# A hand-ordered attention and MLP kernel: loads of q, k, v and f shared between the DMA queues of SyncE and GpSimd, with a new order

## The chip, the cores and the metric

The kernel runs on one core of one Trainium2 chip. The metric is the device time of one execution in microseconds. A program is handed to the five engines as five instruction streams, each executed in order: TensorE (PE), VectorE (DVE), ScalarE (ACT), GpSimd (POOL) and SyncE (SP, which here only issues transfers). Semaphores tie the streams together. Transfers issued by SP go through one queue (q1 in the profile, hardware_dynamic), those issued by POOL through another (q0, software_dynamic); both are carried by the core's 16 transfer engines.

## What is computed

A gated linear attention (a state per head that decays by a sigmoid of f and takes in an outer product of k and v), and then an MLP with SiLU on its result:

```python
batch, n_heads, seq, head_dim = (4, 8, 768, 48)
f = 1.0 / (1.0 + np.exp(-f_logit))
for t in range(S):
    state = f[:, :, t, :, None] * state + np.einsum('bhd,bhe->bhde', k[:, :, t], v[:, :, t])
    y[:, :, t] = np.einsum('bhd,bhde->bhe', q[:, :, t], state)
x = y.transpose(0, 2, 1, 3).reshape(B * S, H * D)          # 3072 x 384
h = x @ w_in                                               # 384 -> 2048
out = (h * (1.0 / (1.0 + np.exp(-h)))) @ w_out             # 2048 -> 384
```

All inputs and the output are float32; the matmuls run in bfloat16.

## The kernel before

The sequence is cut into chunks of 128 steps, so there are 4 batches with 6 chunks each, 24 units. Two units are worked on together as a pair; there are twelve pairs, numbered P in the order of the list `PAIRS`. Pairs 0 to 3 hold chunks 0 and 1 of one batch (form T: a partition holds two neighbouring steps, so that a run in memory is 2 x 48 floats, 384 bytes). Pairs 4 to 11 hold the same chunk of two batches (form N: a run is 48 floats, 192 bytes). A load brings one of q, k, v, f for a whole pair, 384 KB, or half of it: 1024 runs for a T pair, 2048 for an N pair.

Within a chunk the recurrence is done by matmuls. E and L (ACT) make the logarithm of the gate from f, `cs` (PE) its running sum by a triangular matrix, `a`, `ia` and `al` (ACT) exponentials of it, `qg` and `ki` scaled copies of q and k, `vb` a bfloat16 copy of v. q and k are transposed either on PE (`tq`, copied out by `qkc`) or by a DMA transpose that SP issues (`qkD`). `sc` are the score matmuls, `at` their masking, `y` and `yi` the results from scores and from the state before, `d`, `sd` and `su` the state's update. `yc` copies y out, and y is transposed on PE (`yT`, `xc`) or by a DMA transpose (`yD`). The MLP of a pair has eight groups `mi` of six matmuls of 256 columns, each with a SiLU `si` on ACT, and two times four groups `mo` of four matmuls of 384 columns; `oc` copies a result out of PSUM and `so` stores it. The weights come by four loads `wi` and four `wo`, issued by POOL.

The order of all this on all engines is a written list, `PLAN`. A word such as `q.2.0:S:0` names the step (q), the pair (2), the part (0), the engine (A = ACT, V = DVE, G = POOL, S = SP, P = PE) and, after the second colon, the buffer that the step takes. The words are emitted in the order of the list, so each engine's stream is the list's words for it; nothing is reordered later. A step waits only for the data it reads and for the last use of the buffer that it takes, so a load whose buffer has not been used yet is issued as soon as its engine comes to it. The words `idle.512.n` put n filler matmuls on zeros onto PE (L424).

Every load of q, k, v and f is issued by SP:

```python
            return nc.sync.dma_start(out=dst, in_=src)     # L223
```

Its buffer comes from a pool of its own (`SLOTS`: f 4, k 6, q 6, v 6, of which the list uses two or three each). The first four loads of the list are emitted ahead of everything, then the masks are built on POOL and DVE, then the list follows.

Of the kernel before, what the change touches and what calls it, by code (L numbers as in the profile page):

```python
# [33 lines left out]
SLOTS = dict(f=4, k=6, q=6, v=6, e=2, lf=3, x=5, qk=5, vb=7, qkT=4, qkTT=2, atm=4, yb=3, xT=4, hT=4, sd=2, al=6, ob=6, pb=8, st0=1, st1=1, st2=1, st3=1)  # L34
# [23 lines left out]
at.3.0.0:V:0 si.2.7:A: mo.2.1.2:P: mo.2.1.3:P: vb.5.0:G:2 at.3.1.0:V:1 mo.2.0.0:P:3 mo.2.0.1:P: mo.2.0.2:P: f.4.0:S:1 E.4.0:A:0 sd.3.1:V:0 f.6.0:S:0
qkD.5.1:S:0 at.3.1.1:V: qkD.5.0:S:1 oc.2.1:A:4 L.4.0:A:0 cs.4.1:P:5 E.6.0:A:1 L.6.0:A:1 at.3.0.1:V: v.5.1:S: sc.5.0:P:7,6 y.3:P:0,4 sc.5.1:P:2,1
at.5.0.0:V:2 yi.3.1:P: a.4.1:A:0 yc.3.0:A:0 at.5.1.1:V:0 mo.2.0.3:P: at.5.0.1:V: yc.3.1:A:1 oc.2.0:A:5 al.4.1:A:1 d.5.0:P:0 cs.6.0:P:4 a.6.0:A:1  # L60
# [46 lines left out]
def kernel(  # L107
# [82 lines left out]
    def al_of(P, i):  # L190
        return at("al", P)[:, :, i] if PAIRS[P][0] == "T" else at("al", P, i)[:, :, 0]
# [5 lines left out]
    def emit(kind, rest, eng):  # L197
# [26 lines left out]
        if kind in "EL":  # L224
# [3 lines left out]
            if kind == "E":  # L228
                return nc.scalar.activation(e, at("f", P)[:, j * w:(j + 1) * w], AF.Exp, scale=-1.0)  # L229
# [276 lines left out]
```

## Time and profile before

| what | value |
|---|---|
| time, median of three runs | 181.08 us (178.41 to 182.14) |
| profiled execution: time, span | 178.94 us, 177.2 us |
| PE busy | 170.6 us, 96% |
| ACT busy | 130.4 us, 74% |
| DVE busy | 81.2 us, 46% |
| POOL busy | 62.5 us, 35% |
| moved by the transfer engines | 32.12 MB, 181 GB/s over the span |

The span is the time from the first to the last instruction in the trace; the execution's own time holds 1.7 us more. Matmuls are pipelined and their ends are modelled, so PE's busy time counts overlapping matmuls as busy and says little of how densely they follow each other: starts of neighbouring groups are the better measure. In a table of groups a line holds the source line, the engine, the operation, the number of instructions, the time they were busy and the mean of one in ns, and then the idle time before them and what ended it. In the chain of waits and in a timeline the first column is the start and the second the duration in us. In a view of the transfers a queue's line gives its packets, its megabytes and the time that its packets took as a share of 16 engines' time.

### The profile page before, as it was taken

Reading aid. Unit: us, or ns where it says so; the run is one execution under the profiler, and the core shown is the slowest. Engines: PE = TensorE matmul, PEld = TensorE weight load, DVE = VectorE, ACT = ScalarE, POOL = GpSimd, SP = SyncE. Lnnn points to the kernel's source line nnn. Section 1 sums busy time; section 2 is a strip of 40 time slices with the busy share of each in tenths; the row PEclk is TensorE's granted clock in tenths of the full one; section 3 lists DMA queues with packets and bytes.
Section 4 is the critical chain, followed back from the end, with each engine's and each line's share of the span. In section 5 each row is a group of like instructions: output and inputs, shape, how many; then the busy total and the mean of one; then the engine's idle time right before and its main releaser. Section 6 shows DMA issues by size and latency. Waiting matters only on the chain.

```text
span 177.2 us, 4721 instructions
## 1 busy us (share of the span) xinstructions
PE 170.6 (96%) x1912; PEld 124.7 (70%) x1915; DVE 81.2 (46%) x165; ACT 130.4 (74%) x241; POOL 62.5 (35%) x105
## 2 busy tenths in 40 slices
PE   6998999999999999999999999999999999999991
PEld 2446688666886788766787687686797686877860
DVE  7089751047795783125777174035770152520110
ACT  3968578953999989998499788899589574281721
POOL 6056593102383348400647323400471960000001
PEclk9999999999999999999999999999999999999999
DMA  5999999999999989997698796899968998132202
GB/s 145 301 311 256 213 225 204 188 179 237 218 196 201 211 177 199 219 204 151 135 231 152 148 228 141 213 192 212 234 129 191 212 150 242 48 91 87 93 0 89
DMA packets 110453, 32.12 MB, mean 181 GB/s; under 512 B 104080, under 2 KB 110256, under 8 KB 110432
## 3 DMA queue, kind: packets, MB, share of 16 engines
q1 hardware_dynamic: 106432, 27.89, 76.2%
q0 software_dynamic: 4000, 3.93, 12.2%
q8 instruction: 15, 0.25, 0.6%
q14 instruction: 6, 0.05, 0.1%
HBM read 25.17 MB, written 4.72 MB: 169 GB/s over the span
## 4 chain that ended last, share of the span: by engine, by line
PE 74%; ACT 9%; DVE 6%; DMA 4%; SPq 3%; issue 2%; DVEq 0%; ACTq 0%
PE pb L279 32%; PE pb L244 27%; DVE qk L312 3%; DMA q<-in_q_dram 3%; ACT hT L249 3%; PE pb L340 2%; ACT L473 2%; ACT x L307 2%; PE pb L352 2%; PE pb L356 2%; PE pb L336 1%; SPq L368 1%; DMA out_dram<-ob 1%; SPq L223 1%; PE pb L364 1%
## 5 line engine op out<-in xcount | busy, mean ns | idle before, releaser
L244 PE MATMUL pb<-xT,w_in_sb 128*128 128x256 bf16 x576 | 69.3, 272 | 0.5 <-ACT ob L180 0.2
L279 PE MATMUL pb<-w_out_sb,hT 128*128 128x384 bf16 x384 | 68.5, 326 | 0.0
L244 PEld LDWEIGHTS <-w_in_sb 128*128 128x128 bf16 x576 | 54.9, 98 | 9.6 <-issue 1.2
L249 ACT ACTIVATE hT<-pb 128x512 bf16<-128x512 f32 x96 | 50.5, 610 | 10.7 <-PE pb L244 10.5
L279 PEld LDWEIGHTS <-hT 128*128 128x128 bf16 x384 | 36.2, 98 | 21.0
L383 POOL TENSOR_TENSOR st<-sd,al 48x192 bf16<-48x192 f32 x40 | 21.7, 543 | 56.8 <-PE pb L352 34.2
L344 DVE TENSOR_TENSOR atm<-pb,triu 128x512 bf16<-128x512 f32 x32 | 20.1, 684 | 11.2 <-PE pb L340 6.6
L307 ACT ACTIVATE x<-pb 128x384 f32<-128x384 f32 x48 | 21.1, 497 | 5.2 <-PE pb L295 3.1
L473 ACT ACT_TABLE_LOAD x17 | 21.8, 1283 | 0.3
L182 DVE COPY ob<-pb 128x384 f32<-128x384 f32 x10 | 5.4, 552 | 26.6 <-PE pb L279 26.6
L377 DVE TENSOR_TENSOR sd<-pb,st 128x384 f32<-128x384 f32 x16 | 8.8, 553 | 11.8 <-PE pb L373 10.3
L312 POOL TENSOR_TENSOR qk<-k,x 128x384 bf16<-128x384 f32 x11 | 12.0, 1102 | 5.5 <-ACT x L307 2.4
L312 POOL TENSOR_TENSOR qk<-q,x 128x384 bf16<-128x384 f32 x11 | 10.9, 997 | 8.5 <-ACT x L307 5.5
L229 ACT ACTIVATE e<-f 128x768 f32<-128x768 f32 (+1 forms) x13 | 10.2, 792 | 4.8 <-DMA f<-in_f_logit_dram 4.8
L180 ACT COPY ob<-pb 128x384 f32<-128x384 f32 x14 | 6.7, 482 | 9.0 <-PE pb L279 8.2
L312 DVE TENSOR_TENSOR qk<-q,x 128x384 bf16<-128x384 f32 x13 | 8.6, 682 | 7.7 <-DMA q<-in_q_dram 4.2
L289 POOL DMA_DIRECT2D out_dram<-ob x3 | 1.7, 562 | 28.5 <-DVE ob L182 28.5
L424 PE MATMUL pb<-zero,triu 128*128 128x512 bf16 (+1 forms) x27 | 9.8, 463 | 1.5 <-POOL triu masks.py:66 1.4
L344 DVE TENSOR_TENSOR atm<-pb,mask 128x512 bf16<-128x512 f32 x16 | 10.2, 684 | 2.1 <-PE pb L336 1.0
L182 POOL CAST vb<-v 128x384 bf16<-128x384 f32 x12 | 6.5, 551 | 10.9 <-DMA v<-in_v_dram 10.5
L182 DVE CAST yb<-pb 128x384 bf16<-128x384 f32 x14 | 7.6, 555 | 5.4 <-PE pb L356 2.8
L180 ACT CAST yb<-pb 128x384 bf16<-128x384 f32 x10 | 4.8, 490 | 5.8 <-PE pb L356 4.3
(71 smaller groups left out, 148.8 us busy)
## 6 DMA issues: line engine op xcount, KB each, us to landing
f<-in_f_logit_dram SPq DMA_DIRECT2D x11, 384.0 KB, 5.2
k<-in_k_dram SPq DMA_DIRECT2D x10, 384.0 KB, 5.2
q<-in_q_dram SPq DMA_DIRECT2D x10, 384.0 KB, 5.4
v<-in_v_dram SPq DMA_DIRECT2D x10, 384.0 KB, 5.3
out_dram<-ob SPq DMA_DIRECT2D x13, 192.0 KB, 2.1
w_in_sb<-in_moe_w_in_dram POOLq DMA_DIRECT2D x4, 384.0 KB, 8.4
w_out_sb<-in_moe_w_out_dram POOLq DMA_DIRECT2D x4, 384.0 KB, 10.3
out_dram<-ob SPq DMA_DIRECT2D x14, 96.0 KB, 3.5
```

The costliest lines, as they stand in the source:

```text
L180: nc.scalar.copy(dst, src)
L182: ENG[eng].tensor_copy(dst, src)
L229: return nc.scalar.activation(e, at("f", P)[:, j * w:(j + 1) * w], AF.Exp, scale=-1.0)
L244: nc.tensor.matmul(h[:, i, cols], w_in_sb[:, kk, n * 128:(n + 1) * 128], at("xT", P)[:, kk, cols], start=(kk == 0), stop=(kk == KT - 1))
L249: return nc.scalar.activation(at("hT", P)[:, 2 * j:2 * j + 2, :], at("h", P, j).rearrange("p (n c) -> p n c", n=2), AF.Silu)
L279: nc.tensor.matmul(o, at("hT", P)[:, n, i * C:(i + 1) * C], w_out_sb[:, n, :], start=(n == 0), stop=(n == NT - 1))
L307: nc.scalar.activation(at(kind, P, i).rearrange("p h d -> p (h d)"), at("cs", P, i)[:, 0:HD], AF.Exp, scale=1.0 if kind == "ia" else -1.0)
L312: ENG[eng].tensor_mul(at("qk", P, i)[:, j, :, 0:D], heads("qk"[j], P, i), at("ia" if j else "a", P, i))
L344: ENG[eng].tensor_mul(at("atm", P, i)[:, r], at(f"s{r}", P, i).rearrange("p (n c) -> p n c", c=C), mask[:, None, :].to_broadcast([C, NP, C]))
L383: nc.gpsimd.tensor_mul(at("st", P, i)[lo:lo + D, :, r * D:(r + 1) * D], at("sd", P, i)[lo:lo + D, :, r * D:(r + 1) * D], al_of(P, i)[lo:lo ...
L424: nc.tensor.matmul(buf["pb", int(got)][:, 0:rest[0]], triu, zero[:, 0:rest[0]], start=True, stop=True, skip_group_check=True)
L473: nc.scalar.preload_act_table_set(turns[n])
```

## The change

All q, k, v and f loads take buffers from one pool of 24 (`inp`), and each word of the list says whether SP or POOL issues it. Of 55 such loads and halves of loads SP now issues 29 and POOL 26. The exponential E is written over f itself instead of a buffer e. The masks and the identity (`mk`, `mv`) and the column sums of the gates (`on`, formerly part of `cs`) are words of the list of their own. The state update `su` may run on DVE and does so for fourteen of twenty. Pairs 0 and 1 begin in the opposite order, POOL issues the most urgent loads of the first three pairs and the weights between them, and SP issues loads of later pairs from early on. PE's transposes `yT` fall from fifteen to six and DMA transposes `yD` rise from nine to eighteen. There are 24 filler matmuls (16 of 512 columns, 8 of 256) instead of 30 (26 and 4). POOL issues twelve of the 24 results' stores instead of four. Further words (`aD`, `ir`, a DMA transpose for T pairs) are defined and not used by this list.

The core of the diff (of the list: the beginnings, the stretch around the first N pairs, and the end):

```diff
-SLOTS = dict(f=4, k=6, q=6, v=6, e=2, lf=3, x=5, qk=5, vb=7, ...)
+SLOTS = dict(inp=24, lf=3, x=5, qk=5, vb=7, ...)
 PLAN = """
-f.1.0:S:0 E.1.0:A:0 L.1.0:A:0 idle.512.10::0 idle.256.1::0 cs.1.1:P:0 f.0.1:S:1 f.0.0:S: E.0.0:A:1 E.0.1:A: k.1.0:S:0 L.0.0:A:1 L.0.1:A: idle.512.1::1 cs.1.0:P:1
-q.1.0:S:0 idle.512.2::2 cs.0.0:P:2 idle.256.1::3 cs.0.1:P:3 a.1.1:A:0 qg.1.1:V:0 a.1.0:A:1 ia.1.1:A:2 ki.1.1:V: idle.512.1::4 tq.1.1:P:4 ia.1.0:A:3
-ki.1.0:V:1 v.1.0:S:0 f.2.0:S:0 qg.1.0:V: idle.512.3::5 tq.1.0:P:1 vb.1.1:V:0 vb.1.0:G:1 d.1:P:5,6 qkc.1.1:V:0 qkc.1.0:V: idle.512.1::7 idle.256.1::7
-sc.1.0:P:1,4 at.1.0.0:V:0 ia.0.0:A:0 k.0.0:S:1 ki.0.0:V:0 at.1.0.1:V: idle.512.2::7 idle.256.1::7 sc.1.1:P:7,1 at.1.1.0:V:1 at.1.1.1:V: a.0.1:A:2
-ia.0.1:A:3 sd.1.0:A:0 wi.1:G: al.1:A:0 E.2.0:A:1 L.2.0:A:1 q.0.0:S:1 a.0.0:A:1 qg.0.0:V: idle.512.1::5 cs.2.0:P:0 cs.2.1:P:5 al.2:A:1 ia.2.1:A:0
-su.1.0:G:0 ia.2.0:A:4 al.0:A:2 a.2.0:A:1 qg.0.1:V:1 idle.512.2::2 y.1:P:1,7 tq.0.0:P:4 v.0.0:S:1 yc.1.0:V:0 a.2.1:A:2 qkc.0.0:A:1 sd.1.1:V:0 wi.3:G:
-ki.0.1:G: tq.0.1:P:3 qkc.0.1:V: yT.1.0:P:1 yi.1.1:P: yc.1.1:A:0 wi.0:G: idle.512.2::2 sc.0.1:P:3,4 vb.0.1:G:0 at.0.1.0:V:0 yT.1.1:P:7 xc.1.0:A:0
-sc.0.0:P:6,5 at.0.0.1:V:1 at.0.0.0:V: vb.0.0:A:1 wi.2:G: idle.512.1::2 d.0:P:3,1 xc.1.1:A: sd.0.0:A:1 su.0.0:G:0 mi.1.2:P:7 mi.1.3:P:3 at.0.1.1:V:
-...
+f.0.1:S:0 E.0.1:A: f.0.0:S: E.0.0:A: L.0.0:A:0 L.0.1:A: f.1.0:G:1 E.1.0:A: L.1.0:A:1 mk.1:G: mk.0:G: mv.0:V: idle.512.9::0 idle.256.1::0 cs.0.1:P:0
+idle.256.1::1 cs.0.0:P:1 idle.256.1::2 on.0:P: idle.256.1::2 cs.1.0:P:2 cs.1.1:P:3 on.1:P: f.2.0:S:2 E.2.0:A: ia.1.0:A:0 a.1.0:A:1 L.2.0:A:1
+idle.512.4::4 cs.2.0:P:2 cs.2.1:P:4 q.1.0:G:3 qg.1.0:V:0 ia.1.1:A:2 k.1.0:G:4 a.1.1:A:1 ia.0.0:A:3 al.1:A:0 a.0.0:A:4 f.4.0:G:5 E.4.0:A: ki.1.0:V:
+mk.2:G: tq.1.0:P:5 ki.1.1:V:1 qg.1.1:V: on.2:P: tq.1.1:P:3 qkc.1.0:V:0 qkc.1.1:V: idle.512.2::6 idle.256.1::6 sc.1.0:P:3,5 ia.0.1:A:1 L.4.0:A:1
+al.0:A:1 a.0.1:A:2 k.0.0:G:0 v.1.0:G:1 vb.1.1:A:0 vb.1.0:A:1 al.2:A:2 sc.1.1:P:1,6 cs.4.0:P:7 cs.4.1:P:0 on.4.1:P: on.4.0:P: q.0.0:G:6 ki.0.1:V:2
+ia.2.1:A:1 wi.1:G: at.1.0.1:V:0 v.0.0:G:4 at.1.0.0:V: a.2.1:A:0 idle.512.1::5 d.1:P:3,5 sd.1.0:A:0 qg.0.1:V: wi.0:G: ki.0.0:G:3 k.2.0:G:5 ia.2.0:A:2
+tq.0.1:P:4 qkc.0.1:A:1 a.2.0:A:3 qg.0.0:G: tq.0.0:P:3 at.1.1.0:V:1 at.1.1.1:V: y.1:P:6,1 yc.1.0:A:0 su.1.0:V:0 yi.1.1:P: qkc.0.0:V: idle.256.1::4
+sc.0.0:P:3,4 yc.1.1:A:1 sd.1.1:V:0 idle.256.1::2 yT.1.0:P:6 idle.256.1::2 yT.1.1:P:1 q.2.0:G:1 wi.2:G: at.0.0.1:V:0 vb.0.1:G:0 xc.1.0:V:0 at.0.0.0:V:
+al.4.0:A:3 sc.0.1:P:5,2 at.0.1.1:V:1 at.0.1.0:V: vb.0.0:A:1 d.0:P:4,6 xc.1.1:A: mi.1.2:P:1 mi.1.3:P:3 wi.3:G: y.0:P:5,2 f.3.0:S:7 E.3.0:A: sd.0.0:A:1
+al.4.1:A:4 su.0.0:V:0 L.3.0:A:1 sd.0.1:V:1 yi.0.1:P: wo.0:G: yc.0.0:A:1 ki.2.0:V:2 yc.0.1:A:0 ia.4.1:A:4 cs.3.1:P:4 on.3:P: al.3:A:5 yT.0.0:P:5
+xc.0.0:A:1 yT.0.1:P:2 mi.1.0:P:6 xc.0.1:V: ki.2.1:G:3 su.0.1:G:0 a.4.1:A:2 wo.1:G: q.4.1:S:8 qg.2.0:V: wo.2:G: a.3.1:A:1 f.6.0:S:9 wo.3:G: mi.1.1:P:5
+q.7.0:G:5 qg.4.1:V:0 k.5.1:G:7 qg.2.1:V: tq.2.0:P:0 ia.3.1:A:3 qkc.2.0:V:1 k.4.0:S:10 k.6.0:G:1 mi.0.0:P:2 v.3.0:S:11 ia.4.0:A:2 tq.2.1:P:4 a.4.0:A:0
+...
+qkc.3.1:V:1 a.5.1:A:1 mi.2.4:P:6 mi.2.1:P:7 qg.5.1:V:3 v.4.1:S: k.11.0:G:13 ki.5.1:G: al.5.1:A:2 v.8.0:S:20 oc.0.1:V:3 E.9.0:A: mi.2.7:P:4 si.2.1:A:0
+qkc.3.0:V: si.2.6:A: mi.2.0:P:0 mi.2.2:P:7 si.2.4:A: mi.2.3:P:6 si.2.7:A: si.2.2:A: mi.2.5:P:4 si.2.0:A: sc.3.0:P:7,2 at.3.0.1:V:0 at.3.0.0:V:
+sc.3.1:P:0,5 si.2.3:A: si.2.5:A: mo.2.1.0:P:6 mo.2.1.1:P: mo.2.1.2:P: d.4.0:P:7 v.5.1:S: vb.5.1:G:1 L.9.0:A:0 L.7.0:A:1 f.10.0:S:21 at.3.1.1:V:1
+a.5.0:A:2 k.7.0:G:16 at.3.1.0:V: d.3:P:5,2 y.3:P:0,4 yc.3.0:A:0 sd.4.0:V:1 v.9.0:S:22 cs.9.0:P:7 a.9.0:A:1 v.6.0:S:23 mo.2.1.3:P: oc.2.1:A:4
+cs.7.1:P:0 sd.3.0:V:0 su.3.0:V:0 sd.3.1:V:0 yi.3.1:P: cs.7.0:P:3 on.7.1:P: on.7.0:P: on.9.0:P: mo.2.0.0:P:2 vb.5.0:G:2 qg.6.0:V:2 d.5.1:P:6
+qkD.5.1:S:0 yc.3.1:A:1 sc.5.1:P:4,5 mo.2.0.1:P: mo.2.0.2:P: su.3.1:V:0 a.6.1:A:0 ki.5.0:G:4 E.8.0:A: L.8.0:A:1 ki.6.0:G: a.7.1:A:3 at.5.1.0:V:0
+yD.3.0:S:1 qg.6.1:V:3 qg.5.0:G: al.7.1:A:5 ia.7.1:A:0 mo.2.0.3:P: oc.2.0:A:5 yD.3.1:S: qkD.4.1:S:1 ia.6.1:A:2 at.5.1.1:V: sd.5.1:V:0 vb.6.0:V:3
+y.5.1:P:5 yc.5.1:A:1 qkD.5.0:S:2 su.5.1:V:0 ia.7.0:A:4 yD.5.1:S:0 al.6.1:A:2 d.5.0:P:0 vb.8.0:G:4 ki.6.1:G: ki.7.1:G:4 sd.5.0:V:0 cs.9.1:P:6 so.2.1:S:
+mi.3.2:P:4 mi.3.0:P:2 si.3.0:A:0 mi.3.4:P:1 mi.3.3:P:0 on.9.1:P: mi.3.1:P:5 qkD.4.0:S:0 vb.8.1:V:1 si.3.2:A: q.9.0:S:1 si.3.4:A: si.3.3:A: mi.3.6:P:2
+si.3.1:A: si.3.6:A: mi.3.5:P:1 si.3.5:A: mi.3.7:P:0 si.3.7:A: vb.7.0:V:5 mo.3.1.0:P:5 qkD.6.1:S:3 sc.5.0:P:1,2 at.5.0.1:V:0 at.5.0.0:V: sc.4.1:P:0,4
+so.1.1:G: mo.3.1.1:P: mo.3.1.2:P: y.5.0:P:1 yc.5.0:A:1 vb.4.1:G:6 su.5.0:G:0 cs.8.1:P:2 on.8.1:P: at.4.1.0:V:1 mo.3.1.3:P: at.4.1.1:V: y.4.1:P:4
+...
+si.10.2:A:0 si.11.6:A: mo.11.0.1:P: mi.10.4:P:4 mo.11.0.2:P: mo.11.0.3:P: oc.11.0:A:0 so.11.0:G: mi.10.3:P:1 si.10.3:A: mo.11.1.2:P: mo.11.1.3:P:
+mi.10.5:P:1 si.10.0:A: si.10.1:A: mo.10.1.0:P:6 mi.10.7:P:2 mo.10.1.1:P: mo.10.0.0:P:0 mi.10.6:P:3 si.10.4:A: oc.11.1:A:3 so.11.1:G: si.10.5:A:
+si.10.7:A: mo.10.0.1:P: mo.10.1.2:P: si.10.6:A: mo.10.1.3:P: oc.10.1:A:3 so.10.1:S: mo.10.0.2:P: mo.10.0.3:P: oc.10.0:A:0 so.10.0:S:
 """
...
-            return nc.sync.dma_start(out=dst, in_=src)
+            return ENG[eng].dma_start(out=dst, in_=src)
...
-            e = at("e", P)[:, j * w:(j + 1) * w]
+            e = at("f", P)[:, j * w:(j + 1) * w]
             if kind == "E":
-                return nc.scalar.activation(e, at("f", P)[:, j * w:(j + 1) * w], AF.Exp, scale=-1.0)
+                return nc.scalar.activation(e, e, AF.Exp, scale=-1.0)
...
+        if kind == "mk":
+            if rest[0] == 2:
+                return make_identity(nc, ident)
+            return make_upper_triangular(nc, tstrict if rest[0] else triu, 1.0, diag=not rest[0])
...
-                nc.gpsimd.tensor_mul(at("st", P, i)[lo:lo + D, :, r * D:(r + 1) * D], ...
+                ENG[eng].tensor_mul(at("st", P, i)[lo:lo + D, :, r * D:(r + 1) * D], ...
...
-                nc.tensor.matmul(buf["pb", int(got)][:, 0:rest[0]], triu, zero[:, 0:rest[0]], start=True, stop=True, skip_group_check=True)
+                nc.tensor.matmul(buf["pb", int(got)][:, 0:rest[0]], zero[:, 0:C], zero[:, 0:rest[0]], start=True, stop=True, skip_group_check=True)
...
-        loads = [t for t in plan if t[0] in SRC][:4]
-        for t in loads:
-            run(*t)
-        make_upper_triangular(nc, triu, 1.0, diag=True)
...
```

More of the change, by code (lines that the diff above doesn't have):

```diff
@@ L249, in emit @@
             return nc.scalar.activation(at("hT", P)[:, 2 * j:2 * j + 2, :], at("h", P, j).rearrange("p (n c) -> p n c", n=2), AF.Silu)
+        if kind == "on" and T:
+            lf, cs = at("lf", P), at("cs", P, 1)
+            for p in range(NP):
+                for j in range(2):
+                    nc.tensor.matmul(cs[:, HD + 2 * p:HD + 2 * p + 2], lf[:, j, 2 * p:2 * p + 2, :], halves,
+                                     start=False, stop=(j == 1), skip_group_check=True)
+            return
         if kind == "al" and T:
@@ L331, in emit @@
                 if T:
-                    both = at("qkT", P)
                     for r in range(2):
@@ L388, in takes @@
     def takes(kind, rest):
-        if kind in ("wi", "wo", "so", "yi", "idle"):
+        if kind in ("wi", "wo", "so", "yi", "on", "E", "idle", "mk", "mv"):
             return []
@@ L473 @@
                 nc.scalar.preload_act_table_set(turns[n])
-            if t not in loads:
-                run(*t)
+            run(*t)
 _INS = ['q', 'k', 'v', 'f_logit', 'moe_w_in', 'moe_w_out']
```

194 lines of the change are left out of this document (91 added, 103 removed).

## The prediction

> **What bounds the kernel now.** I read the page first, then PE's waits, then the chain of waits and PE's timeline, and last the transfers in windows.
>
> ```profile
> span 177.2 us, 4721 instructions
> PE 170.6 (96%) x1912; PEld 124.7 (70%) x1915; DVE 81.2 (46%) x165; ACT 130.4 (74%) x241; POOL 62.5 (35%) x105
> DMA  5999999999999989997698796899968998132202
> ```
> ```profile
> PE pb L424 <- POOL triu masks.py:66: 1.4, 1, 1.4
> PE pb L258 <- DVE atm L344: 0.6, 1, 0.6
> ```
> ```profile
> 1.37 4.66 PE L424 MATMUL pb<-zero,triu 128*128 128x512 bf16 x11 [1.37 <-POOL triu masks.py:66]
> ...
> 7.32 0.59 PE L424 MATMUL pb<-zero,triu 128*128 128x512 bf16 x2
> 7.76 0.32 PE L295 MATMUL pb<-lf,tincl 128*128 128x384 bf16 x1
> ...
> 20.10 1.48 PE L244 MATMUL pb<-xT,w_in_sb 128*128 128x256 bf16 x12
> ```
> ```profile
> 23.36 8.52 PE pb L244 x78
> 31.88 4.55 PE pb L279 x28
> ...
> 59.04 0.33 PE pb L340 x8
> ...
> 82.44 0.55 PE pb L340 x16
> ...
> 168.95 4.56 PE pb L279 x28
> 173.58 0.48 ACT ob L180
> ```
>
> PE is the bound. Its longest waits are 1.4 and 0.6 us, both early, and 78 first-layer matmuls take 8.52 us, 0.109 each; 28 second-layer ones 4.55, 0.163 each. From the first MLP group at 20.1 us to the last matmul at 173.5 PE runs almost without a hole. What remains is the start (20.1 us, partly filler of L424) and the tail (177.2 - 173.5 = 3.7 us). The second resource is the transfer engines: the DMA row stands at 9 in most slices until about 140 us. So there are two questions: does PE get less work, and does every load still land before PE asks for it?
>
> **PE's work.** Group prices come from start to start:
>
> ```profile
> 84.88 0.33 PE L352 MATMUL pb<-st,qkT 128*128 128x96 bf16 x4
> 85.05 0.36 PE L356 MATMUL pb<-vb,atm 128*128 128x48 bf16 x8
> 85.26 0.32 PE L302 MATMUL pb<-lf,triu 128*128 128x384 bf16 x1
> 85.42 0.24 PE L305 MATMUL pb<-ones,lf 128*128 128x1 bf16 x4
> 85.52 0.33 PE L352 MATMUL pb<-st,qkT 128*128 128x96 bf16 x4
> ...
> 86.54 0.33 PE L373 MATMUL pb<-vb,qk 128*128 128x96 bf16 x4
> 86.71 0.33 PE L364 MATMUL pb<-ident,yb 128*128 128x128 bf16 x3
> 86.88 0.33 PE L302 MATMUL pb<-lf,triu 128*128 128x384 bf16 x1
> ```
>
> The plan drops nine of fifteen PE transposes yT (0.17 each, 1.5 us) for nine more DMA transposes yD on SP, which run in the second half of the kernel, where the DMA row falls to 0 to 3 towards the end; the tq, sc, y, d, mi and mo groups stay as many. Fillers fall from 26 wide and 4 half-wide ones to 16 and 8; they fill holes and save nothing by themselves. Fourteen of twenty state updates su (two instructions each) move from POOL to DVE; at no more than POOL's two times 0.5 us each they are 15 us there, hidden by DVE's idle half (81.2 of 177.2 us busy); without that cover they would delay the next pair's scores by 1 us each. The tail is the same: ACT copies, SP stores. If all data arrived in time, the change would be worth 1.5 us and whatever the start gains.
>
> **The moved transfers.** A load of a T pair (first two chunks) is 1024 packets of 384 bytes, one of an N pair 2048 packets of 192. Four windows of the transfers, 4 to 8 us, 38 to 39, 21 to 24 and 31 to 35:
>
> ```profile
> DMA packets 3205, 1.21 MB, mean 302 GB/s; under 512 B 3205, under 2 KB 3205, under 8 KB 3205
> q1 hardware_dynamic: 3205, 1.21, 111.9%
> ```
> ```profile
> q1 hardware_dynamic: 1085, 0.21, 101.6%
> q0 software_dynamic: 10, 0.00, 3.1%
> ```
> ```profile
> q0 software_dynamic: 446, 0.44, 86.2%
> q1 hardware_dynamic: 462, 0.18, 32.5%
> ```
> ```profile
> q0 software_dynamic: 761, 0.56, 90.1%
> q1 hardware_dynamic: 763, 0.17, 34.6%
> ```
>
> Alone, SP's queue moves 3205 T packets in 4 us, so a T load costs 1.28 us of all engines; 1085 N packets in 1 us make an N load 1.89 us. With weights of POOL's queue under way both queues advance packet for packet (446 to 462, 761 to 763). Four w_in loads of 384 packets then take 10.3 us and four w_out loads of 512 take 10.8; SP moves 1.6 T loads and 1 N load meanwhile (3.9 us), so the weights by themselves cost 17.2.
>
> In the changed order SP meets no buffer that holds it up at first (24 shared slots; a queue's ninth DMA waits for its first), so it runs into loads that are needed late, while POOL issues the urgent ones. SP's transpose for the scores of pair 5 (sc.5.1) stands behind 7 T and 14 N loads in SP's queue. POOL has by then issued 9 T loads, 11 N loads (halves added up) and the weights. The kernel before reaches its first N scores at 59.0 us having needed only 16 T loads, about 8 N loads and the weights. PE's work ahead of that point is alike, so PE could be there at 59.
>
> What two queues of small packets do together the trace doesn't show. From both sides:
> - The engines' time simply adds up: 16 x 1.28 + 25 x 1.89 + 17.2 + 1.1 for the transpose (1024 small packets) = 86.1; with 1.5 before the first packet and 2 to land, 89.6 us.
> - Per-packet cost is hidden by the other queue and only bytes count, at the highest read rate of the trace: from 21 to 24 us 446 reads of 2 KB and 462 of 384 bytes, 1.09 MB in 3 us, 363 GB/s. 41 loads of 0.393 MB and 6.29 MB of weights are 22.4 MB: 61.7, with 1 and 3.5 as above 66 us.
>
> I take the middle, 78, since neither row is nearer. From sc.5.1 to PE's end stand 72 mi of six matmuls (0.655), 75 mo of four (0.65), 16 sc (0.275), 16 y (0.38), 10 d (0.17), 7 cs (0.16) and 3 column sums (0.10): 47.2 + 48.8 + 4.4 + 6.1 + 1.7 + 1.1 + 0.3 = 109.6. The span is then 78 + 109.6 + 3.7 = 191.3, and with the 1.7 us around it (178.94 of the profiled execution less 177.2) 193.0 us. That execution lies 1.2% below the median of 181.08. The ends are 181.0 (66) and 204.6 (89.6).
>
> The same sum at two earlier places shows where the loss begins.
>
> ```profile
> 17.68 0.50 POOL L182 CAST vb<-v 128x384 bf16<-128x384 f32 x1 [1.48 <-DMA v<-in_v_dram]
> ```
>
> v of pair 0, which d.0 and with it the first MLP group wait for, lands at 17.6 now. In the new order POOL has 7 T loads, 1 N load and one w_in load up to it, and SP moves as many packets besides (4 T and 2.5 N loads): 6.5 MB, 20.6 us by bytes; by addition 14.1 + 6.6 + 2.6 and 2.7 around it, 26. And cs.5.0 needs f.5.0, the fourteenth DMA of SP: 5 T and 5.5 N loads of SP beside 9 T, 1 N and the weights of POOL, 44 us by bytes and 51 by addition. PE could be there at 38 (20.1 and 16 mi, 6 mo and 3.4 us of small groups). PE's queue is strictly in order, so the MLP groups behind cs.5.0 cannot fill that hole. Both delays are contained in the 78.
>
> The Trainium skill, "DMA: Bandwidth & Descriptors", section "Issuing engines are not separate DMA queues", says that DMAs of all issuing engines run on the same 16 engines and that several issuers save only issue time. By it the adding end, 204.6, would hold; the windows above agree with shared engines, but show no pair of small streams.
>
> **POOL's own time.** An issue there occupies the engine:
>
> ```profile
> L202 POOL DMA_DIRECT2D w_in_sb<-in_moe_w_in_dram x4 | 3.4, 844 | 0.0
> L205 POOL DMA_DIRECT2D w_out_sb<-in_moe_w_out_dram x4 | 3.2, 792 | 0.0
> L289 POOL DMA_DIRECT2D out_dram<-ob x3 | 1.7, 562 | 28.5 <-DVE ob L182 28.5
> ```
>
> 128 packets cost 0.56, 448 on average 0.82: 0.8 ns for each more. A T load is then 1.3 us, an N load 2.1; in plain proportion to w_in (2.2 ns a packet) 2.25 and 4.5. Until ki.5.1, which the transpose of pair 5 needs, POOL has 13 issues of 1024 packets, 8 of 2048, 6.5 us of weights and some 14 us of multiplies, casts and masks: 54 us at the low price, which just fits, 86 at the high one. I take the low, since the rows have a large fixed part. Behind each issue that waits, POOL's multiplies and state updates wait too.
>
> **Rivals.**
> - Two queues of small packets pass each other without loss, and loads land as fast as they are issued. Then v.0.0 lands by 17 and f.5.0 by 36, no hole opens, and 1.5 us of transposes and 2 us of the start are gained: 178.9 - 3.5 = 175.4. For it: each queue alone is busy for 100 to 112%, about one packet at a time, which leaves room for a second. Against it: beside the weights SP's queue fell from 801 or 1085 packets a microsecond to 154 and 191. It ends on the other side, and decides once all loads up to f.5.0 move in 35 us.
> - Bytes alone count (66 us): 181.0, no change.
> - PE starts slowly again after a hole. The first eleven fillers take 0.42 us each, two later ones 0.22, so the slow start cost 2.3 us; two such holes would add 4.6 to the forecast: 197.6. Against it: no later hole of before is long enough to show it.
> - POOL's issues are the bound at the high price: 86 us and 2.5 to transpose, then the 109.6, 3.7 and 1.7: 203.5.
> - The sharing does nothing, because POOL's loads come through only as SP's do: the same packets pass, about 193 as well, so it has no chance of its own.
>
> The Trainium skill, "TensorE: Matmul & The Clock Gate", Part 1, says that an idle window of about 3.4 us halves PE's clock until PE has been busy as long. By it the third rival holds, with 3.4 us for two holes; the slow first fillers agree.
>
> **How the numbers follow.** Forecast, SP's queue reaches pair 5 late: 0.45 (185 to 205). Slow restarts on top: 0.18. POOL's issues: 0.10. Bytes: 0.12. No loss: 0.15. About 2% is what a measurement of this kernel can tell from no change, 177.5 to 184.7 around the median. The first two and POOL's case are slower by more; bytes alone stay within, no loss is faster: faster 0.15, within 0.12, slower 0.73. The range, 176 to 206, leaves out most of the first rival and the upper end of the third and fourth; the forecast's own is 185 to 205.
>
> **What would show it.** Right: PE waits of several us at L318 or L320 (cs) near 40 to 50 us, ended by ACT after a late f, and at the score matmuls of pair 5 (L367) near 60 to 80, ended by a DMA transpose; queue q0 with some 45,000 packets; the first MLP group after 22 us; dense PE afterwards, 110 us before the end. Wrong: PE dense from 20 us on, sc.5.1 near 60 us, or a joint rate above 363 GB/s with both queues at small packets.

## The result, and the profile after

The changed kernel takes 219.34 us (median of 4 runs, 216.67 to 220.22) against 179.75 for the kernel before (4 runs beside it): a ratio of 1.224 [1.210, 1.238]. It is 22% slower, where the prediction said 7% and gave a range that ends at 206.

The page of the changed kernel: span, engines, granted clock and transfers in 40 slices, and the two queues (packets, MB, share of 16 engines' span). The last two lines are the same queues on the page of the kernel before.

```profile
span 217.5 us, 4641 instructions
PE 180.9 (83%) x1882; PEld 127.7 (59%) x1882; DVE 91.2 (42%) x188; ACT 128.4 (59%) x241; POOL 77.2 (36%) x103
PEclk9887999955766799999999958999999999999999
DMA  6999999999999999169699990163493715112011
q1 hardware_dynamic: 68624, 17.77, 42.6%
q0 software_dynamic: 7328, 14.95, 29.8%
```
```profile
q1 hardware_dynamic: 106432, 27.89, 76.2%
q0 software_dynamic: 4000, 3.93, 12.2%
```

The shares times the spans are the engines' own time: 72.4% of 217.5 is 157.5 us after, 88.4% of 177.2 is 156.6 before. Sharing out the loads saved the engines nothing in sum (nine more transposes are in it), though POOL's queue now carries 11 MB more in only 3,300 packets more. PE, nearly gapless before, has four holes of over 4 us. Its waits, and its timeline at these places (start, duration, idle time before it and what ended it):

```profile
PE pb L302 <- DVE atm L371: 9.8, 1, 9.8
PE pb L260 <- DMA xT<-yb: 6.5, 1, 6.5
PE pb L320 <- ACT lf L252: 4.5, 1, 4.5
PE pb L320 <- DVE atm L371: 4.1, 1, 4.1
```
```profile
24.07 1.48 PE L260 MATMUL pb<-xT,w_in_sb 128*128 128x256 bf16 x12
...
49.21 5.46 PE L302 MATMUL pb<-w_out_sb,hT 128*128 128x384 bf16 x20 [9.78 <-DVE atm L371]
59.22 0.48 PE L320 MATMUL pb<-lf,triu 128*128 128x384 bf16 x1 [4.54 <-ACT lf L252]
...
67.67 0.48 PE L320 MATMUL pb<-lf,triu 128*128 128x384 bf16 x1 [4.14 <-DVE atm L371]
...
91.60 0.40 PE L367 MATMUL pb<-qkT 48*128 48x128 bf16 x8
...
126.39 2.72 PE L260 MATMUL pb<-xT,w_in_sb 128*128 128x256 bf16 x12 [6.48 <-DMA xT<-yb]
```

The first MLP group starts at 24.07 (20.10 before), cs.5.0 at 59.2, the scores of pair 5 (sc.5.1) at 91.6 with no wait ahead of them, and 125.9 us follow to the end. Behind a hole PE is slow: after the first one, 20 second-layer matmuls take 5.46 us, 0.273 each instead of 0.163, where the clock row shows 5.

What the first three holes waited for is seen on DVE and ACT:

```profile
48.01 0.55 DVE L179 CAST vb<-inp 128x384 bf16<-128x384 f32 x1 [16.96 <-DMA inp<-in_v_dram]
...
66.46 0.56 DVE L336 TENSOR_TENSOR qk<-inp,x 128x384 bf16<-128x384 f32 x1 [16.70 <-DMA inp<-in_q_dram]
```
```profile
57.45 0.84 ACT L245 ACTIVATE inp<-inp 128x768 f32<-128x768 f32 x1 [16.76 <-DMA inp<-in_f_logit_dram]
```

In the first hole PE waits to write mo.0.0.0 into a buffer that the mask at.2.0.1 still has to read. In DVE's list this mask stands behind vb.4.0, the cast of a later pair, which waits for v.4.0 until 48.0 us. In the second, cs.5.0 waits for f.5.0. In the third, cs.5.1 waits for a buffer of the mask at.2.1.1, which stands behind qg.3.1 and its q.3.0. All three loads are SP's. How SP's queue fares is seen in SP's issues, in POOL's wait, and in the transfers from 59 to 61 us:

```profile
11.21 14.97 SPq L239 DMA_DIRECT2D inp<-in_k_dram  x1
...
33.45 9.60 SPq L239 DMA_DIRECT2D inp<-in_v_dram  x1
...
81.94 1.33 SPq L355 DMA_TRANSPOSE qkT<-qk  x1
...
117.64 8.30 SPq L355 DMA_TRANSPOSE qkT<-qk  x2
```
```profile
47.36 0.99 POOL L336 TENSOR_TENSOR qk<-inp,x 128x384 bf16<-128x384 f32 x1 [13.22 <-DMA inp<-in_q_dram]
```
```profile
q0 software_dynamic: 117, 0.41, 95.6%
q1 hardware_dynamic: 117, 0.02, 10.0%
```

117 packets of each queue pass in 2 us, but POOL's carry 0.41 MB and SP's 0.02. A POOL packet holds 3.5 KB on average, some 18 runs of 192 bytes (22 in the largest, 4,224 bytes), an SP packet one run. While POOL has anything outstanding, SP's queue gets one run for about twenty of POOL's; its issues are held for 15 and 10 us. Late q.4.0, one of SP's, holds POOL's multiply for 13.2 us, and with it every load that POOL would issue behind it. Whether the starved queue costs time in sum is tested below (e1).

The transpose for the scores of pair 5 is the line at 81.94. SP has issued the loads ahead of it by 77.6 us, it leaves when POOL has finished ki.5.1, and it lands at most 3.5 us later, 6 us before PE comes to the scores. The last line shows two transposes held for 8.3 us; the two xT issued just ahead of them, from 113.9 us on beside three loads of POOL, land only at 126.3, where the fourth hole ends.

The Trainium skill, "DMA: Bandwidth & Descriptors", section "Queues, rings and completion order", says that an engine changes queues only between packets, and that a packet typically drains 9 to 17 descriptors of one queue. The 117 to 117 packets agree with the turns; the 22 runs in POOL's and the single run in SP's are what these traces add.

### The profile page after: what moved, and what is told of

Its sections match the earlier page's. It is cut to its first block, busy times and chain, and to the rows that moved or that the text cites. A ratio compares the mean times of both kernels' runs of the same rounds, so it can differ in the third digit from the quotient of the medians.

```text
span 217.5 us, 4641 instructions
## 1 busy us (share of the span) xinstructions
PE 180.9 (83%) x1882; PEld 127.7 (59%) x1882; DVE 91.2 (42%) x188; ACT 128.4 (59%) x241; POOL 77.2 (36%) x103
## 4 chain that ended last, share of the span: by engine, by line
PE 53%; DMA 20%; SPq 17%; DVE 6%; issue 1%; POOL 0%; ACT 0%; DVEq 0%; POOLq 0%
PE pb L260 24%; PE pb L302 22%; SPq L239 16%; DMA inp<-in_q_dram 14%; DMA xT<-yb 6%; DVE atm L371 2%; DVE st L414 2%; PE pb L367 2%; PE pb L383 1%; PE pb L387 1%; DMA out_dram<-ob 1%; PE pb L320 1%; DVE sd L408 1%; SPq L399 1%; POOL qk L336 0%
## 5 line engine op out<-in xcount | busy, mean ns | idle before, releaser
L302 PE MATMUL pb<-w_out_sb,hT 128*128 128x384 bf16 x384 | 76.6, 348 | 9.8 <-DVE atm L371 9.8
L336 POOL TENSOR_TENSOR qk<-inp,x 128x384 bf16<-128x384 f32 x22 | 22.9, 1043 | 64.9 <-ACT x L329 43.3
L336 DVE TENSOR_TENSOR qk<-inp,x 128x384 bf16<-128x384 f32 x26 | 16.9, 663 | 29.1 <-DMA inp<-in_q_dram 16.7
L245 ACT ACTIVATE inp<-inp 128x768 f32<-128x768 f32 (+1 forms) x13 | 10.3, 794 | 20.3 <-DMA inp<-in_f_logit_dram 20.2
L179 DVE COPY ob<-pb 128x384 f32<-128x384 f32 x12 | 6.6, 553 | 23.9 <-PE pb L302 23.3
L414 DVE TENSOR_TENSOR st<-sd,al 48x192 bf16<-48x192 f32 x28 | 13.1, 467 | 1.9 <-PE pb L383 0.9
L320 PE MATMUL pb<-lf,triu 128*128 128x384 bf16 x16 | 5.8, 371 | 8.7 <-ACT lf L252 4.5
L179 DVE CAST vb<-inp 128x384 bf16<-128x384 f32 x9 | 4.0, 457 | 17.0 <-DMA inp<-in_v_dram 17.0
L414 POOL TENSOR_TENSOR st<-sd,al 48x192 bf16<-48x192 f32 x12 | 6.7, 559 | 11.6 <-DVE sd L408 5.8
L455 PE MATMUL pb<-zero 128*128 128x512 bf16 (+1 forms) x24 | 9.1, 494 | 1.8 <-DVE halves L477 1.2
L239 POOL DMA_DIRECT2D inp<-in_k_dram x9 | 9.6, 1070 | 0.2 <-issue 0.2
```

What stands on the lines that cost most here:

```text
L179: ENG[eng].tensor_copy(dst, src)
L239: return ENG[eng].dma_start(out=dst, in_=src)
L245: return nc.scalar.activation(e, e, AF.Exp, scale=-1.0)
L302: nc.tensor.matmul(o, at("hT", P)[:, n, i * C:(i + 1) * C], w_out_sb[:, n, :], start=(n == 0), stop=(n == NT - 1))
L336: ENG[eng].tensor_mul(at("qk", P, i)[:, j, :, 0:D], heads("qk"[j], P, i), at("ia" if j else "a", P, i))
L414: ENG[eng].tensor_mul(at("st", P, i)[lo:lo + D, :, r * D:(r + 1) * D], at("sd", P, i)[lo:lo + D, :, r * D:(r + 1) * D], al_of(P, i)[lo:lo ...
```

## The experiments

Times are medians of four or more runs; the ratio is to the kernel before beside them. Words of the list are shown as kind.pair.part:engine (S is SP, G is POOL). "Pair 5" is the start of the first score matmuls of pair 5 on PE in the profiled execution (sc.5.1; in the kernel before sc.5.0), "rest" what is left of its span from there. The four runs of f5 spread from 211.0 to 222.3 us, and the profiled one is the fastest of them.

| kernel | us | ratio | pair 5 | rest |
|---|---|---|---|---|
| before | 179.7 | 1 | 59.0 | 118.2 |
| changed | 219.3 | 1.224 [1.210, 1.238] | 91.6 | 125.9 |
| e1 all loads on SP | 217.7 | 1.199 [1.186, 1.213] | 96.0 | 119.0 |
| e2 last four of POOL on SP | 212.1 | 1.172 [1.161, 1.184] | 93.7 | 117.0 |
| e3 nine more on POOL | 226.0 | 1.249 [1.239, 1.259] | 100.2 | 124.7 |
| f1 by first use, shared | 208.9 | 1.166 [1.153, 1.179] | 87.9 | 119.3 |
| f2 by first use, all SP | 211.1 | 1.178 [1.168, 1.189] | 90.3 | 118.5 |
| f3 by first use, all POOL | 209.8 | 1.168 [1.152, 1.183] | 90.7 | 119.4 |
| f4 f2, sixteen behind | 211.2 | 1.179 [1.168, 1.190] | 74.3 | 135.0 |
| f5 f1, sixteen behind | 215.4 | 1.200 [1.181, 1.219] | 74.1 | 135.1 |
| f6 changed, sixteen behind | 223.0 | 1.240 [1.227, 1.254] | 82.0 | 138.1 |
| f7 f5, last four on SP | 214.6 | 1.195 [1.187, 1.204] | 74.0 | 139.0 |
| g1 changed, long runs | 200.5 | 1.111 [1.101, 1.121] | 73.3 | 124.1 |
| g2 before, long runs | 181.1 | 1.009 [1.005, 1.014] | 61.7 | 117.7 |
| b1 before, loads shared | 225.9 | 1.257 [1.240, 1.273] | | |
| b2 before, nine yD | 206.2 | 1.145 [1.135, 1.154] | | |
| h1 changed, holes filled | 217.7 | 1.208 [1.198, 1.219] | 91.9 | 124.0 |
| i1 changed, nine back on PE | 216.1 | 1.203 [1.192, 1.214] | 92.7 | 121.5 |
| i2 f4, nine back on PE | 203.7 | 1.130 [1.114, 1.147] | 73.9 | 128.4 |

**The streams by themselves (m1).** Loads of both forms and DMA transposes in stages, with fences between them.

> This kernel computes nothing of the reference: it only runs streams of loads in stages, with a fence between them, and stores zeros. Stages: six N loads on SP; six on POOL; six on each at once; four DMA transposes on SP; six N loads on POOL with four DMA transposes on SP; six T loads on SP; six on POOL. Theory 'turns' (POOL's queue packs some 20 runs into a packet of up to 4,224 bytes, SP's carries one run of 192 or 384, and the 16 engines change from queue to queue packet by packet): SP alone 12,288 packets of 192 bytes at about 1,100 a microsecond, 11 us; POOL alone only some 600 packets of about 4 KB and 6 to 8 us; both at once, SP's queue passes about as many packets as POOL's while POOL has work (100 a microsecond or fewer, not 1,100) and then the rest alone, 17 to 19 us in all, POOL's loads landing first; the transposes, some 4 to 5 us alone, take 6 to 8 us longer beside POOL's loads. Rival 'engine times add': both queues advance evenly by work, SP's loads and POOL's loads land together, and POOL's packets are as small as SP's.

SP's N loads alone (4 to 14 us), POOL's alone (20 to 28), both (37 to 45, two lines):

```profile
q1 hardware_dynamic: 11607, 2.21, 116.9%
```
```profile
q0 software_dynamic: 496, 1.76, 103.7%
```
```profile
q0 software_dynamic: 466, 1.65, 96.7%
q1 hardware_dynamic: 491, 0.09, 10.2%
```

Alone, SP moves 221 GB/s and POOL 220: POOL's large packets are no faster per load. Together they move 1.74 MB in 8 us, 218 GB/s, 466 packets to 491, nearly all of it POOL's. The stage of twelve loads began at 30.4 us. The reads on DVE behind it, when SP's first two and its last loads are there:

```profile
34.11 0.15 DVE L56 COPY seen<-inp 128x1 f32<-128x1 f32 x1 [3.38 <-DMA inp<-in_q_dram]
47.36 0.15 DVE L56 COPY seen<-inp 128x1 f32<-128x1 f32 x1 [13.10 <-DMA inp<-in_k_dram]
...
53.90 0.77 DVE L56 COPY seen<-inp 128x1 f32<-128x1 f32 x7 [1.27 <-DMA inp<-in_k_dram]
```

Twelve loads take 23.5 us, 1.96 each, where 17 to 19 in all was expected: the times add, and SP's second load waits 13 us for POOL's queue to run empty. The eight transposes of the kernel, four alone (2.3 to 2.5 us) and four beside POOL's loads, landed between 2.3 and 11.9 us after their issue:

```profile
DMA to landing us min/median/max: 2.3/2.7/11.9
```

Both theories were half right: the sum adds, and the turns decide who is late.

**Queues (e1, e2, e3).** In the changed list: all 26 `:G:` loads to `:S:` (e1); only q.11.0, q.8.0, k.8.0, k.10.0 to `:S:` (e2); q.4.1, k.4.0, v.3.0, q.4.0, k.4.1, v.2.0, f.5.0, k.3.0, q.3.0 to `:G:` (e3).

> The changed kernel with all 26 loads that POOL issues given back to SP at the same place of the list; weights stay on POOL. Theory 'turns' (SP's queue passes one small packet for each large one of POOL's, so SP's loads starve): the list's order stays, but nothing of SP is starved except beside the weights; the first scores of pair 5 come at the adding end of the prediction, about 85 us, there is no hole at 120 to 126 us, and the time is 195 to 207. Rival 'order' (the list loads things early that are needed late, whatever the queue): holes of the same kind, 213 to 222. Rival 'POOL's issue time and its waits hold the kernel back': 26 issues of about 1 us leave POOL, its multiplies come earlier, and the time falls to 185 or less.

> The changed kernel with only the last four loads of POOL (q.11.0, q.8.0, k.8.0, k.10.0) given to SP at the same place of the list. Theory 'turns': the transposes yD.4.0 and yD.6.1, which took from 113.9 to 126.4 us beside three POOL loads, land within 3 us; PE's wait of 6.5 us at L260 goes, with the slow clock behind it: 209 to 213, and nothing changes before 110 us. Rival 'the engines are simply full there' (the same bytes pass in the same stretch): 217 to 221.

> The changed kernel with nine of SP's loads that PE waited for (q.4.1, k.4.0, v.3.0, q.4.0, k.4.1, v.2.0, f.5.0, k.3.0, q.3.0) given to POOL at the same place of the list. Theory 'turns': they now travel in large packets; POOL's hold-up at qg.4.0 (34 to 47 us) goes because q.4.0 is there; the holes of 9.8, 4.5 and 4.1 us before 68 us shrink to less than 8 in all; 195 to 207. Rival 'engine times add': the same work passes the same engines, and 217 to 221 stays. Rival 'POOL's issue time': nine more issues on POOL make it later, over 222.

e1 is above what the theory of the turns gave, and where the rival 'order' had it. Without a starved queue the same three holes stand (8.9, 3.6 and 3.6 us), since v.4.0, f.5.0 and q.3.0 are there at 49.2, 58.0 and 66.5 us, no earlier than in the change (48.0, 57.5, 66.5). The scores of pair 5 come at 96.0, and now they do wait for their transpose:

```profile
50.24 5.98 PE L302 MATMUL pb<-w_out_sb,hT 128*128 128x384 bf16 x20 [8.91 <-DVE atm L371]
...
95.99 0.40 PE L367 MATMUL pb<-qkT 48*128 48x128 bf16 x8 [3.35 <-DMA qkT<-qk]
```

In sum the sharing costs next to nothing here. e2 came as expected: the hole at 120 us goes and the rest falls from 125.9 to 117.0. There SP's transposes stood beside POOL's loads. e3 missed its 195 to 207: more in the favoured queue made it later still, in the range of the rival 'POOL's issue time' (over 222). What its trace shows is a wait more than issue time: f.5.0, which SP issued at 48.6 us, leaves POOL at 57.4, behind a multiply that waited 9.7 us for q.4.0, and the hole at cs.5.0 grows from 4.5 to 13.7 us.

**Order (f1, f2, f3).** The loads dealt to the same places of the list by first use; queues of the change, all SP, all POOL.

> The changed kernel with the same loads on the same queues (26 on POOL, 29 on SP) at the same places of the list, but dealt out to these places in the order in which they are first used (the list had some of them up to 26 places away); slots of the 24 dealt anew. Theory 'order' (engine times add whatever the queue; the loss comes from loads needed late that stand ahead of loads needed early): the holes before 68 us, 18 us and some 8 us of slow clock, mostly go: 183 to 195. Theory 'turns' (SP's queue starves beside POOL's large packets, so whatever is on SP comes late): SP's early loads still starve, holes of over 10 us before 70 us stay: 200 to 216.

> The same order by first use, and all 55 loads on SP; weights on POOL. Both theories: no starvation and the right order, 178 to 190. If it stays above 205, neither order nor sharing is the cause, but something in the other engines' streams.

> The same order by first use, and all 55 loads on POOL. Theory 'order': the loads take the engines as long as on SP (1.8 us an N load, by the streams alone), so only POOL's in-order waits and some 57 us of issue time count against it: 185 to 205, worse than on SP alone. Theory 'turns': loads do not starve each other, but SP's transposes beside them take 10 us and more: 190 to 210.

All three lie between 208.9 and 211.1: order by need is worth 7 to 10 us, the queue nothing. f1 and f3 lie in the ranges of 'turns', but without its early holes; f2 was put at 178 to 190 by both theories and misses by 21 us. In f2 PE runs almost without a hole from its first MLP group to 73 us, and then:

```profile
90.25 0.61 PE L364 MATMUL pb<-qkT 48*128 48x128 bf16 x8 [17.15 <-DMA qkT<-qk]
```

Its transpose stands behind the same loads as before and leaves SP only at 85.6 us. (In f3 it leaves at 68.4, and takes 22.2 us beside POOL's loads.) Seven kernels with the same loads ahead of it reach the scores of pair 5 at 88 to 100 us, whatever the order and the queue. In e1, f1, f2 and f3 the scores wait for the transpose (3.4 to 17.2 us); in the change, e2 and e3 the transpose is there first, and the earlier holes have made PE late.

**Fewer loads ahead (f4 to f7).** Sixteen loads (q.7, k.6, k.9, v.10, f.8, f.11, v.7, k.5.0, q.5.0, v.4.1, k.11, v.8, f.10, k.7, v.9, v.6) put behind qkD.5.1; f7 also has e2's four on SP.

> Sixteen loads whose first use stands in the list behind the transpose for the scores of pair 5 (qkD.5.1), but which were issued ahead of it, go behind it; the others in order of first use; all loads on SP. Theory 'volume ahead' (the engines' times add, whoever issues: 89.6 us for 67.7 us of loads, 17.2 of weights, 1.1 of the transpose and 3.5 around them; the five kernels so far reach the scores of pair 5 at 88 to 100 us): 27.4 us less stand ahead, so the transpose could be through at 62 and PE, which starts its first MLP group near 26 us and has 47 us of work, comes to the scores of pair 5 at 73 to 77 with no hole of over 4 us before: 186 to 196. Rival (the streams of the other engines hold PE, not the loads): the scores of pair 5 stay behind 85 us, 204 or more.

> As the kernel with the sixteen loads behind the transpose and the others by first use, but on the queues of the change (SP and POOL). Volume ahead: the scores of pair 5 at 73 to 78, 186 to 198. If the turns of the queues (SP passes one small packet for one large one of POOL's) are a loss of their own beside the volume: at 80 or later, over 200.

> The changed kernel with nothing but these sixteen loads moved behind the transpose of pair 5; the others at their places, in the change's order and on its queues. Volume ahead: 27.4 us less ahead, the scores of pair 5 at 73 to 80 instead of 91.6, and 193 to 205; the late hole at 120 us may stay. Rival 'turns': SP's loads needed early (f.5.0, q.3.0, q.4.0) still starve beside POOL's, and the scores stay behind 85: 208 or more.

> The shared kernel with the sixteen loads behind and the others by first use, and with q.11.0, q.8.0, k.8.0 and k.10.0 on SP, behind the transposes they ran against. By the earlier run that moved these four alone (7.2 us less): 4 to 8 us below the shared kernel, 180 to 192. If nothing is left of the late hole once the loads come earlier: the same as the shared kernel within 2 us.

```profile
74.25 0.40 PE L364 MATMUL pb<-qkT 48*128 48x128 bf16 x8
...
81.82 4.23 PE L257 MATMUL pb<-xT,w_in_sb 128*128 128x256 bf16 x24 [4.40 <-DMA xT<-yb]
...
101.28 1.44 PE L257 MATMUL pb<-xT,w_in_sb 128*128 128x256 bf16 x6 [5.30 <-DMA xT<-yb]
```

In f4, f5 and f7 the scores of pair 5 came when the volume ahead said (f4: 74.3 for 73 to 77), but the times did not follow: 211 to 223, where 180 to 205 was expected. What was gained ahead was given back behind: from f2 to f4 the rest grew from 118.5 to 135.0, 9.7 us of it in waits for transposes xT, which now share SP's queue with the moved loads. f6, which keeps the other loads in the change's order, keeps a first hole of 8.3 us, reaches pair 5 at 82.0 and is later than the change. f7's four loads saved nothing (214.6, with f5 between 211.0 and 222.3).

**Loads made cheap (g1, g2).** `src` of every load of q, k, v, f is a contiguous piece of the same size.

> The changed kernel, but every load of q, k, v, f reads as many bytes from contiguous memory (runs of 3 KB or 1.5 KB instead of 192 or 384 bytes), so its values are other ones; queues, order and every other instruction are those of the change. Theory 'the loads' engine time' (the new compute order asks for loads earlier than 16 engines deliver small runs): with loads about half as dear the holes go, 175 to 186. Rival 'the other engines' streams or the transposes hold PE': the holes stay at least by half, 198 or more.

> The kernel before with the same contiguous reads. PE has no holes to close after its start, so at most the start moves: 174 to 180 under either theory. The difference between this and the changed kernel with contiguous reads is what the change costs or gains when loads are no bound: 1.5 us of gain by the transposes if the prediction's sum of PE's work was right.

The changed kernel gains 19 us, far from the 175 to 186 of 'the loads' engine time' and within the rival's 198 or more; the kernel before does not gain, and lies just above its 174 to 180. So about half of the loss goes with the small runs (by e1 with the engines' time for them, not with the turns), and about 19 us (200.5 against 181.1) do not. The early holes shrink to 3.0 and 1.5 us. In g1 the first MLP group still starts late, and the late hole is still there, with SP's two transposes held for 8.3 us:

```profile
24.47 1.48 PE L261 MATMUL pb<-xT,w_in_sb 128*128 128x256 bf16 x12
...
107.34 2.72 PE L261 MATMUL pb<-xT,w_in_sb 128*128 128x256 bf16 x12 [6.01 <-DMA xT<-yb]
```
```profile
98.58 8.32 SPq L356 DMA_TRANSPOSE qkT<-qk  x2
```

**Parts of the change in the kernel before (b1, b2).** b1: the 26 loads to `:G:`, `ENG[eng].dma_start` at L223. b2: `yT.P.i:P` dropped and `xc.P.i` made `yD.P.i:S` for pairs 3, 4, 5, 9 and 6.1.

> The kernel before, with the same 26 loads given to POOL that the change gives it, each at its old place of the list; nothing else changed. Sharing by itself. Theory 'order': the total work of the engines is the same and the old order nearly by need, so little changes beyond POOL's issue time: 178 to 192. Theory 'turns': SP's remaining loads starve whenever POOL's are under way: 195 to 215.

> The kernel before with only the nine PE transposes turned into DMA transposes that the change turns (pairs 3, 4, 5, 9 and the second half of pair 6). By the prediction's sum 1.5 us less, 177 to 180. Rival 'a DMA transpose in SP's in-order queue stands behind loads and holds the MLP groups that wait for it' (the changed kernel's wait of 6.5 us at 120 us): slower, 183 to 195.

Both are slower than even their rivals had it: alone, b1 costs more than the whole change and b2 two thirds of it. In b1 SP issues nothing from 17 to 41.8 us, since its next load waits 23.3 us for one of k that POOL brings in; POOL's issues stand in order behind its state updates:

```profile
SPq L223 <- DMA k<-in_k_dram: 23.3, 1, 23.3
```
```profile
28.79 1.08 POOL L383 TENSOR_TENSOR st<-sd,al 48x192 bf16<-48x192 f32 x2 [3.65 <-ACT sd L180]
...
35.02 0.95 POOL L223 DMA_DIRECT2D k<-in_k_dram  x1
...
51.10 1.08 POOL L383 TENSOR_TENSOR st<-sd,al 48x192 bf16<-48x192 f32 x2 [11.95 <-DVE sd L182]
52.13 0.96 POOL L223 DMA_DIRECT2D q<-in_q_dram  x1
```

In b2 SP stands at a yD until its y is copied, and the loads behind it leave late; two rows of SP and three of PE:

```profile
107.25 1.29 SPq L368 DMA_TRANSPOSE xT<-yb  x1
...
110.56 1.80 SPq L223 DMA_DIRECT2D f<-in_f_logit_dram  x1
```
```profile
99.15 3.63 PE L244 MATMUL pb<-xT,w_in_sb 128*128 128x256 bf16 x18 [3.50 <-DMA xT<-yb]
117.91 0.48 PE L302 MATMUL pb<-lf,triu 128*128 128x384 bf16 x1 [5.63 <-ACT lf L236]
151.77 1.04 PE L340 MATMUL pb<-qkT 48*128 48x128 bf16 x16 [4.80 <-DMA qkT<-qk]
```

The nine transposes save PE 1.5 us of work and cost 26.

**The clock (h1).** `idle.512.44::1` ahead of mo.0.0.0, `idle.512.20::3` ahead of cs.5.0, `idle.512.28::3` ahead of mi.4.3. A filler clears a buffer that is still to be read, so some values are others.

> The changed kernel with filler matmuls on PE in three of its four holes (44 wide ones before the hole of 9.8 us, 20 before that of 4.5, 28 before that of 6.5), nothing else. Theory 'slow restarts' (PE's clock falls after a hole; PE was busy 10.3 us longer than before): PE's work after the holes runs at full clock, 211 to 216. If the clock does not matter or the fillers themselves delay the work behind them: 218 to 222.

```profile
PEclk9878899999995699999999999999999999999999
```
```profile
50.13 3.41 PE L302 MATMUL pb<-w_out_sb,hT 128*128 128x384 bf16 x20 [0.91 <-DVE atm L371]
...
59.38 0.32 PE L320 MATMUL pb<-lf,triu 128*128 128x384 bf16 x1 [1.52 <-ACT lf L252]
```

Across the filled holes the clock stays up, and the 20 matmuls take 3.41 instead of 5.46 us. But cs.5.0 still starts at 59.4, because its f is no earlier, and cs.5.1 at 67.8, because q.3.0 is no earlier: the unfilled hole ahead of it grows from 4.1 to 6.1 us, and behind it the clock row falls to 5 and 6. The next hole swallowed most of what the slow clock cost: 217.7, within the spread of the changed kernel and between the two ranges.

**The nine back on PE (i1, i2).** `yD.P.i:S` made `yT.P.i:P` and `xc.P.i:V` or `:A`. Two of them (3.1, 4.1) read a buffer that a later y has filled by then, so values are others and PE may wait for that copy.

> The changed kernel with its nine additional DMA transposes (pairs 3, 4, 5, 9, second half of 6) turned back into PE transposes with a copy on DVE or ACT; loads, queues and order as in the change. Theory 'transposes in SP's queue' (the same nine alone cost 26.5 us in the kernel before): the wait of 6.5 us at 120 us goes, with its slow clock, PE does 1.5 us more: 205 to 213. Rival: only the kernel before suffers from them, because there the loads stand behind them in SP's queue; in the changed kernel SP's loads are issued by 78 us: 217 to 222.

> All loads on SP, by first use, sixteen of them behind pair 5's transpose (the kernel of 211 us whose scores of pair 5 came at 74 us), and the nine transposes back on PE. Theory 'transposes and loads in one in-order queue': that kernel's later holes ended at DMA transposes xT (9.7 us) and at loads behind them (q at 97, k at 130); without the nine they mostly go: 188 to 200. If it stays above 205, the compute order of the change itself (what PE, ACT and DVE ask for and when) costs more than the queues do.

In the changed kernel they give back 3 us, in f4 7 us; both times lie between the two ranges that were expected. With sharing, the order of the loads, the volume ahead and the transposes all undone 203.7 are left.

## Why the prediction was wrong

**Direction and mechanism.** The direction was right, and so was the kind of mechanism: PE loses time to loads that land late because all loads share the engines. It was not right about the place. The prediction let PE stand at the scores of pair 5 until their transpose lands; in the changed kernel the transpose is there 6 us before PE. That wait shows once the early holes are closed (f1 to f3), and in f2 the scores start at 90.2 us, where the adding end had 89.6. That the changed kernel's 91.6 lies near this end too is luck.

**The step that failed first: what holds PE ahead of pair 5.** "Both delays are contained in the 78" was wrong. They were v.0.0 and f.5.0; that DVE's list has vb.4.0 and qg.3.1 ahead of the masks that free PE's buffers was put at nothing. PE left its third hole at 67.7 and then had 23.9 us of work up to 91.6. The prediction's own prices, added over all loads that stand ahead in the list on either queue, would have found the place. They give 49.6 us for v.4.0 (13 T and 6.5 N loads, the weights at 17.2, and 3.5 around them), 58.5 for f.5.0 (14 and 10.5) and 66.7 for q.3.0 (16 and 13.5); these are estimates made afterwards. DVE and ACT got the three at 48.0, 57.5 and 66.5, and in e1, without sharing, at 49.2, 58.0 and 66.5. For f.5.0 the prediction counted one N load of POOL where the list has five ahead of it.

The middle between two ends failed with it. The transpose of pair 5 was put at 78 us, between 66 (only bytes count) and 89.6 (the engines' times add), and landed near 85. m1 shows why the lower end was none: two queues of small runs move 218 GB/s together, as much as either alone, not 363. That end was taken from 2 KB reads of weights beside short runs. Of the two, the adding end, 204.6, was the forecast to make, as the sentence on the Trainium skill ("DMA: Bandwidth & Descriptors", "Issuing engines are not separate DMA queues") had it.

**The step that failed second: the rest.** It was 109.6 + 3.7 = 113.3 us and measured 125.9. Of the 12.6, 8.9 go with four loads on another queue (e2). Of the other 3.7 some 2 are low prices: by the same prices PE's work behind pair 5 in the kernel before is about 112 us, and took 114.5 there without a hole. The nine transposes were costed at nothing because the transfer row is low late. A transpose that alone lands in 2.3 to 2.5 us takes up to 12 beside POOL's loads, and one that waits for its y holds SP's queue. 13.6 (91.6 less 78) and 12.6 are the 26.2 us by which the span misses its 191.3.

**Other points.** The first MLP group came at 24.07, after 22 as said; cs.5.0 at 59.2 instead of 44 to 51, and not for the starved queue, since e1 has it at 59.8. The wait for a transpose at the scores of pair 5, named as a sign, did not come. The 45,000 packets of q0 were 7,328. "Packet for packet" was right as a rule, but a packet is no run: the same rule made one queue starve. POOL's issues cost less than the low price (0.9 us for a T load, 1.15 for an N load); e1 takes 26 of them away and wins 1.6 us, which is within the spread. PE was not dense to the end.

**The rivals.** No loss and bytes alone fell. Slow restarts were seen, but filling three holes bought 1.6 us. POOL's issues were no bound in the changed kernel (e1), though a load behind a waiting multiply on POOL comes late (e3). "Sharing does nothing" is close for the sum in the new order (e1), and quite wrong for the old one (b1).

**What stays open.** g1 and i2 lie 20 to 24 us above the kernel before. f4, f5, f7, g1 and i2 reach pair 5 at 73 to 74 us without a hole of over 4 us, 14 to 15 us behind the kernel before. In g1, 4.4 us of these are the later first MLP group; PE's short waits and slower work make up the others, and the rest is 5.9 us longer than before, with a hole of 6.0 in it. Why PE's stream is less dense was not tested; fourteen state updates on DVE and the new order on ACT and DVE were never undone. The losses do not add up (e2, f1 and i1 one by one give 7, 10 and 3); in h1 this is because PE's next hole takes up what an earlier one releases. No kernel here beat the kernel before.

## What to carry to other kernels

Two queues are not two sets of engines: price the loads ahead of a point by the sum of their engine time over both queues, and take a lower end only from streams of the same run length. Look for such points on the engines that feed the bound engine or free its buffers too: the largest hole here came from a cast for a later pair, ahead of a mask in DVE's in-order list. An in-order queue that carries loads and transposes should get neither a load that is needed later nor a transpose whose input is late ahead of one that is urgent. A change that keeps the bound engine's work and moves its inputs is judged at each place where that engine asks for data, and a hole closed early is worth only what the next hole leaves.

## What the runs showed of the hardware

POOL's queue packs short runs into packets of 3,456 or 4,224 bytes (384 and 1,920 of them in m1) and SP's does not, and the engines take one packet of each in turn: 466 packets with 1.65 MB against 491 with 0.09 MB in 8 us. The packing brings no speed by itself (220 against 221 GB/s). DMA transposes on SP landed in 2.3 us at best; beside POOL's loads one took 11.9 us in m1 and one 22.2 in f3. With runs of 3 KB the kernel before is not faster (1.009 [1.005, 1.014]), though its transfer row stood at 9 for most of the span.
